# Even weight tiles, second products at the pair's end, and a last output block copied and stored in halves, in a fused GEGLU feed-forward kernel

## The chip, the cores and the metric

The kernel runs on one core of one Trainium2 chip. The metric is the time of one execution on the device in microseconds (us). Times are given as the median of several runs. A profile is one execution recorded by the hardware profiler; its times count from the start of the span.

## The reference

```python
B, S, D, F = 32, 32, 1024, 3584        # all bf16
def _gelu(x):
    return jax.nn.gelu(x, approximate=True)
def reference(x, w_gate, w_up, w_down):   # x: (B, S, D), w_gate and w_up: (D, F), w_down: (F, D)
    return (_gelu(x @ w_gate) * (x @ w_up)) @ w_down
```

With the batch flattened, x has N = 1024 rows. There are two stages: a hidden matrix h of 3584 x 1024 (stored transposed, 28 tiles of 128 rows, in `hT`), and the product with `w_down`.

## The kernel before

**Building blocks.** A small scheduler (`_Program`) collects the instructions of all engines. It works out which instruction must wait for which: by 256-byte cells of the on-chip buffers, and for PSUM by bank. In `add` (line 52) a reader of a PSUM bank also waits for earlier readers of that bank on other engines:

```python
            if key[0] == "ps":
                for d in self.readers.get(key, ()):
                    if d.eng != eng:
                        deps[d.index] = d
```

TensorE (PE) runs its matmuls in the order in which the program lists them. The other engines' instructions, and the DMA issues of each queue, are sorted by a planned time `at`, which is only a sort key: each one then runs as soon as the one before it and the semaphores it waits for allow. All instructions are recorded at one line of the helper `emit` (L117), so the profile's groups are told apart by tile and shape, not by line.

**Stage one.** Gate and up products (j = 0 and 1) are computed for one tile of 128 hidden columns at a time, in two halves of 512 rows of x. After a start phase (four tiles held in `first`, loaded as 1024-byte rows, from tile `F0` = 11), the work goes over 13 pairs p of a left and a right tile (`LEFT`, `RIGHT` = left + 15). Each pair uses a Strassen-like scheme with seven products instead of eight, each with j = 0 and 1, each of four matmuls of 128x128 by 128x512:

- products 1 and 2 use the weights and x as they are (bf16); the others use sums of blocks that VectorE, GpSimd and ScalarE prepare in fp32r (`sums_x` in buffer `S`, `sums_w` in buffer `T`);
- the order in a long pair (p from 4) is 1 1 5 2 2 6 6 5 7 3 7 3 4 4. The short pairs 0 to 3 (`EARLY`) have products 1 and 2 from the start phase (product 1's sums are kept in `kept`, inside tiles of `hT` not yet written) and run 5 5 6 6 7 3 7 3 4 4;
- the eight PSUM banks are A = (0, 1), E = (2, 3), B = (4, 5), C = (6, 7). Product 1 goes to A and is copied by ScalarE to B, where product 6 is added; B is copied to C, where product 7 is added, and so on. Product 5 goes to E and is copied to `p5`;
- GELU is ScalarE's (`act`); the adds and the products that write `hT` are VectorE's (`tt`, `glu`).

Weights of a pair of pairs (a group `gi`) are loaded by SP's queue into `raw[gi % 2]` (`load_pairs`: four DMAs, left and right, gate and up, 512-byte rows). The load of a group waits until all readers of the buffer two groups earlier are done. The last group has one tile on each side, so its rows have 256 bytes. The four `w_down` quarters (`load_wd`) take the place of x and weights later on.

**Stage two.** Seven sweeps of 56 matmuls in the order 1, 2, 7, 5, 6, 3, 4 use the same scheme with tiles 0 to 13 and 14 to 27 of `hT`; sweeps 1 and 2 are bf16, the others fp32r. Sweep 4 ends the kernel: its four blocks t of 128 rows lie in banks 0 to 3 (`PA`), and `done4` (line 554) copies them to `late`, ScalarE for even t and VectorE for odd t, and SP stores each (128 rows of 1024 bytes). SP waits for all stores at the end.

Of the kernel before, what the change touches and what calls it, by code (L numbers as in the profile page):

```python
# [6 lines left out]
P = 128  # L7
# [116 lines left out]
def bass_standalone__geglu_ffn__sampling_kernel(  # L124
# [21 lines left out]
    with ExitStack() as es:  # L146
# [54 lines left out]
        for n in [512] * 6 + [P] * 2:  # L201
            mm(3, one[:, 0:P], one[:, 0:n], True, True)

        NX, F0 = 2, 11
        for i, eng in enumerate(("sp", "act")):
            dma(eng, xn[:, 2 * i:2 * i + 2, :], x_r[:, 2 * i:2 * i + 2, 0:NX * P], 0, f"xn{i}")

        def load_first(eng, j, k0, k1, after=()):
            dma(eng, first[:, j, k0:k1, :], w_r[j][:, k0:k1, F0 * P:(F0 + 4) * P], 0, f"w0_{j}_{k0}", after)

        def load_x(h, k0, k1, after=()):
            pr.add("sp", "dma_start_transpose", xT[h][:, k0:k1, :], xf[h * 512:(h + 1) * 512, k0 * P:k1 * P],
# [17 lines left out]

        LEFT = [11, 12] + list(range(11))
        NP, EARLY = len(LEFT), 4

        def left(p): return LEFT[p]
        def right(p): return LEFT[p] + 15


        kept = [hT[:, m:m + 2, :].rearrange("p t n -> p (t n)").bitcast(FP32).rearrange("p (j n) -> p j n", j=2)  # L240
                for m in (7, 9, 22, 24)]


        SLOT = 0.905
        t0 = 32.7
        T0 = []
        for p in range(NP):
            T0.append(t0)
            t0 += (10 if p < EARLY else 13.9) * SLOT
        base = t0  # L250

        KO = 2
# [1 line left out]
        steps = [(m, j, k) for k in range(DK - KO) for j in range(2) for m in range(4)]  # L254
        for m in range(4):
            steps += [(m, j, k) for j in range(2) for k in range(DK - KO, DK)] + [(m, None, None)]
        for m, j, k in steps:
            if j is None:
                at = 17.0 + m * 0.87
                act(tmp[:, m, :], bank(2 * m), GELU, at)  # L260
                tt(hT[:, F0 + m, 0:512], tmp[:, m, :], bank(2 * m + 1), MUL, at)
                continue
            op = mm(2 * m + j, first[:, j, k, m * P:(m + 1) * P], xT[0][:, k, :], k == 0, k in (3, DK - 1), add=k > 3)
            if k == 3 and m < 2:
                act(kept[m][:, j, :], bank(2 * m + j), COPY, 10.5)
            if (m, j) == (3, 1):
                if k < 2:
                    load_first("act", 0, 2 * k + 4, 2 * k + 6, [op])
                    load_first("act", 1, 2 * k + 4, 2 * k + 6)
                if k == 3:  # L270
                    for k0 in range(0, DK, 2):
                        load_x(1, k0, k0 + 2, [op])
# [5 lines left out]
        for m, j, k in steps:  # L278
            if j is None:
                at = 25.0 + m * 0.87  # L280
                act(tmp[:, m, :], bank(2 * m), GELU, at)
                tt(hT[:, F0 + 2 + m, 512:1024], tmp[:, m, :], bank(2 * m + 1), MUL, at)
                continue
            mm(2 * m + j, first[:, j, k, (m + 2) * P:(m + 3) * P], xT[1][:, k, :], k == 0, k == DK - 1)


        def load_near(at):
# [1 line left out]
                dma("sp", near[:, j, :, :], w_r[j][:, :, right(0) * P:(right(1) + 1) * P], at, f"near{j}")  # L289

        def load_pairs(gi, s, at, ks=slice(0, DK)):
            n = min(2, NP - 2 * gi)
            for j in range(2):
                m = (left, right)[s](2 * gi)
                dma("sp", raw[gi % 2][:, s, j, ks, 0:n * P], w_r[j][:, ks, m * P:(m + n) * P], at, f"w{gi}_{j}{s}_{ks.start}")

        load_near(10)
        load_pairs(1, 0, 11, slice(0, 4))
# [7 lines left out]
        def pair_w(p, s, ks):  # L306
            col = slice((p % 2) * P, (p % 2 + 1) * P)
            if p < 2:
                return first[:, :, ks, col] if s == 0 else near[:, :, ks, col]
            return raw[(p // 2) % 2][:, s, :, ks, col]  # L310


# [53 lines left out]
        sums_w(0, 3, 28.6)  # L366
        t4 = sums_w(0, 4, 33.9)

        A, E, B, C = (0, 1), (2, 3), (4, 5), (6, 7)
        for p in range(NP):  # L370
            t0 = T0[p]
            if p % 2 == 0 and 2 <= p // 2 + 1 < (NP + 1) // 2:
                load_pairs(p // 2 + 1, 0, t0)
                load_pairs(p // 2 + 1, 1, t0)
            if p == 3:
                load_wd(0, 0, t0)
            if p == NP - 1:
                load_wd(0, 1, t0)
            ml, mr = left(p), right(p)
            at = lambda s: t0 + s * SLOT  # L380

            def product(n, j, b, start):
                for k in range(4):
                    if n < 3:
                        kk = k + 4 * (n - 1)
                        l, r = stat(p, j, kk), x0[:, kk, :]
                    else:
                        s, u = {3: (3, 3), 4: (4, 4), 5: (0, 0), 6: (1, 1), 7: (2, 2)}[n]
                        l, r = T[:, unit(p, u), j, k, :], S[:, 4 * s + k, :]
                    mm(b, l, r, start and k == 0, k == 3, add=not start)  # L390

            def glu(m, h, g, u, at_):
                tt(hT[:, m, h * 512:(h + 1) * 512], g, u, MUL, at_)

            p5 = [tmp[:, 0, :], tmp[:, 1, :]]
            g11, g12, g22, g21 = (tmp[:, i, :] for i in range(2, 6))

            if p < EARLY:
                o = -4
                for j in range(2):  # L400
                    act(bank(B[j]), kept[p][:, j, :], COPY, at(0.1 + j * 0.1))
                product(5, 0, E[0], True)
                act(p5[0], bank(E[0]), COPY, at(1))
                product(5, 1, E[1], True)
                product(6, 0, B[0], False)
                act(bank(C[0]), bank(B[0]), COPY, at(3))
                act(p5[1], bank(E[1]), COPY, at(3.1))
                product(6, 1, B[1], False)
                act(bank(C[1]), bank(B[1]), COPY, at(4))
            else:  # L410
                o = 0
                product(1, 0, A[0], True)
                act(bank(B[0]), bank(A[0]), COPY, at(1))
                product(1, 1, A[1], True)
                act(bank(B[1]), bank(A[1]), COPY, at(2))
                product(5, 0, E[0], True)
                act(p5[0], bank(E[0]), COPY, at(3))
                product(2, 0, A[0], False)
                act(g11, bank(A[0]), GELU, at(4))
                product(2, 1, A[1], False)  # L420
                glu(ml, 0, g11, bank(A[1]), at(5.2))
                product(6, 0, B[0], False)
                act(bank(C[0]), bank(B[0]), COPY, at(6))
                product(6, 1, B[1], False)
                act(bank(C[1]), bank(B[1]), COPY, at(7))
                product(5, 1, E[1], True)
                act(p5[1], bank(E[1]), COPY, at(8))
            u22 = bank(A[1] if p < EARLY - 1 else E[1])
            product(7, 0, C[0], False)
            tt(g22, bank(C[0]), p5[0], ADD, at(o + 9.1))  # L430
            act(g22, g22, GELU, at(o + 10))
            product(3, 0, B[0], False)
            tt(g12, bank(B[0]), p5[0], ADD, at(o + 10.1))
            act(g12, g12, GELU, at(o + 11))
            product(7, 1, C[1], False)
            tt(u22, bank(C[1]), p5[1], ADD, at(o + 11.1))
            glu(mr, 1, g22, u22, at(o + 11.9))
            product(3, 1, B[1], False)
            tt(bank(B[1]), bank(B[1]), p5[1], ADD, at(o + 12.1))
            glu(mr, 0, g12, bank(B[1]), at(o + 13))  # L440
            product(4, 0, C[0], False)
            act(g21, bank(C[0]), GELU, at(o + 13))
            product(4, 1, C[1], False)
            glu(ml, 1, g21, bank(C[1]), at(o + 14.1))
            if p + 1 < NP:
                sums_w(p + 1, 0, at(o + 9), "pool", [t4])
                if p + 1 < EARLY:
                    sums_w(p + 1, 1, at(o + 11.5))
                    sums_w(p + 1, 2, at(o + 14.3))
                    sums_w(p + 1, 3, at(o + 9.5))  # L450
                    t4 = sums_w(p + 1, 4, at(o + 14.4))
                else:
                    sums_w(p + 1, 1, at(o + 14.3))
                    sums_w(p + 1, 2, at(o + 12), "pool")
                    sums_w(p + 1, 3, at(o + 9.5))
                    t4 = sums_w(p + 1, 4, at(o + 20.5))


        KL, KR = list(range(14)), list(range(14, FM))
# [92 lines left out]
            out_dma(0, t, 1, late[:, 1, t, :])  # L552

        def done4(t, at):
            if t % 2:
                pr.add("dve", "tensor_copy", late[:, 2, t, :], bank(PA[t]), at=at)
            else:
                act(late[:, 2, t, :], bank(PA[t]), COPY, at)
            out_dma(1, t, 0, late[:, 2, t, :])
# [14 lines left out]
        with nc.Block() as block:  # L574
            for name, e in (("sync", "sp"), ("scalar", "act"), ("gpsimd", "pool"), ("tensor", "pe"), ("vector", "dve")):
                getattr(block, name)(lambda eng, e=e: pr.emit(
                    e, eng, sems, [("out", totals["out"])] if e == "sp" else ()))


# [26 lines left out]
```

## Time and profile before

| what | value |
|---|---|
| median of 7 runs | 276.02 us (275.46 to 276.25) |
| the profiled execution: its own time, its span | 275.69 us, 273.7 us |
| PE busy, matmuls | 270.0 us (99%), 1200 |
| VectorE, ScalarE, GpSimd busy | 189.7, 126.2, 45.5 us |
| granted TensorE clock | full in the whole span |
| matmuls of fp32r sums (S and T) | 800 |
| first fp32r matmul (pair 0) starts at | 32.64 us |
| pair 4 starts, pair 12 ends at | 69.58 us, 183.04 us |
| last matmul ends, last copy ends at | 270.87 us, 271.60 us |
| HBM read | 22.28 MB |

Matmuls are pipelined: the recorded duration of one (some 390 ns) is longer than the distance between two starts, so the length of a stage is read from starts, and a busy PE is not a PE at its peak. PEld are the weight loads that run beside the matmuls. Idle time of another engine costs nothing by itself.

### The profile page before, as it was taken

The page shows a single profiled execution, that of the slowest core. Times are in us where ns is not written, and L with a number is a line of the kernel's source. Part 1 is how long each engine was busy: PE and PEld are TensorE (multiplying, and loading weights), DVE is VectorE, ACT ScalarE, POOL GpSimd, SP SyncE. Part 2 cuts the span into 40 slices and gives each one's busy share as a digit, 9 for nine tenths or more (in the row PEclk, how much of TensorE's full clock was granted, in tenths as well). Part 3 has the DMA queues.
Part 4 walks back from the last instruction along what each step waited for, and adds up shares of the span by engine and source line. Part 5 has one row for each costly group of instructions (what it writes and reads, how often), then busy time and mean ns, then how long its engine had stood idle before and what let it go on. Part 6 is the DMA issues. An engine that isn't in the chain of part 4 may idle for free.

```text
span 273.7 us, 3259 instructions
## 1 busy us (share of the span) xinstructions
PE 270.0 (99%) x1200; PEld 187.4 (68%) x1200; DVE 189.7 (69%) x221; ACT 126.2 (46%) x195; POOL 45.5 (17%) x27
## 2 busy tenths in 40 slices
PE   8999999999999999999999999999999999999995
PEld 4444488888686767767686867674447888888884
DVE  1049978988665648374666666479972999999942
ACT  2353767567464555646454645531120112255561
POOL 1000032035060514325160606000000000000000
PEclk9999999999999999999999999999999999999999
DMA  7999511963800920193400007097011000001112
GB/s 178 275 187 301 134 33 53 282 211 108 199 2 0 244 63 2 39 268 78 78 2 0 0 0 263 7 317 223 0 38 38 0 2 0 0 0 61 38 57 77
DMA packets 46863, 26.42 MB, mean 97 GB/s; under 512 B 12544, under 2 KB 46848, under 8 KB 46848
## 3 DMA queue, kind: packets, MB, share of 16 engines
q1 hardware_dynamic: 44624, 24.25, 33.0%
q10 hardware_dynamic: 2224, 1.97, 2.8%
q8 instruction: 9, 0.15, 0.2%
q14 instruction: 6, 0.05, 0.1%
HBM read 22.28 MB, written 2.10 MB: 89 GB/s over the span
## 4 chain that ended last, share of the span: by engine, by line
PE 99%; DVE 0%; issue 0%
PE ps L117 99%; DVE arena L117 0%
## 5 line engine op out<-in xcount | busy, mean ns | idle before, releaser
L117 PE MATMUL ps<-S,T 128*128 128x512 f32 x520 | 125.5, 397 | 0.0
L117 PEld LDWEIGHTS ps<-S,T 128*128 128x128 f32 x520 | 97.4, 188 | 22.7 <-issue 0.8
L117 POOL TENSOR_TENSOR T<-arena 128x1024 fp32r<-128x1024 bf16 x21 | 44.8, 2152 | 122.4 <-DVE T L117 113.7
L117 ACT ACTIVATE tmp<-ps 128x512 f32<-128x512 f32 x64 | 38.2, 597 | 55.6 <-PE ps L117 55.6
L117 DVE TENSOR_TENSOR hT<-tmp,ps 128x512 bf16<-128x512 f32 x56 | 37.2, 685 | 38.2 <-PE ps L117 35.9
L117 PE MATMUL ps<-arena 128*128 128x512 bf16 x272 | 62.5, 381 | 0.1
L117 ACT ACTIVATE ps<-ps 128x512 f32<-128x512 f32 x52 | 30.3, 584 | 48.4 <-PE ps L117 48.4
L117 PE MATMUL ps<-T,S 128*128 128x512 f32 x224 | 51.3, 390 | 0.0
L117 DVE TENSOR_TENSOR T<-arena,T 128x1024 fp32r<-128x1024 bf16 x40 | 48.4, 1217 | 0.0
L117 PEld LDWEIGHTS ps<-T,S 128*128 128x128 f32 x224 | 42.0, 188 | 8.8
L117 PEld LDWEIGHTS ps<-arena 128*128 128x128 bf16 x272 | 24.8, 98 | 33.6 <-issue 3.4
L117 DVE TENSOR_TENSOR tmp<-ps,tmp 128x512 f32<-128x512 f32 x26 | 18.0, 692 | 21.7 <-PE ps L117 21.7
L117 DVE TENSOR_TENSOR T<-arena 128x1024 fp32r<-128x1024 bf16 x19 | 22.7, 1219 | 7.7 <-PE ps L117 7.4
L117 PE MATMUL ps<-arena,hT 128*128 128x512 bf16 x112 | 24.3, 379 | 0.0
L117 DVE TENSOR_TENSOR ps<-ps,tmp 128x512 f32<-128x512 f32 x30 | 20.9, 696 | 2.8 <-PE ps L117 2.8
L117 PEld LDWEIGHTS ps<-arena,hT 128*128 128x128 bf16 x112 | 10.9, 98 | 13.3 <-issue 0.3
L117 ACT ACTIVATE tmp<-tmp 128x512 f32<-128x512 f32 x26 | 16.4, 632 | 5.7 <-DVE tmp L117 4.6
L117 DVE TENSOR_TENSOR S<-hT 128x1024 fp32r<-128x1024 bf16 x14 | 16.6, 1218 | 0.0
L117 ACT ACTIVATE T<-arena 128x1024 fp32r<-128x1024 bf16 x13 | 13.7, 1053 | 0.0
L117 PE MATMUL ps<-S 128*128 128x512 f32 x56 | 12.9, 389 | 0.0
L117 PEld LDWEIGHTS ps<-S 128*128 128x128 f32 x56 | 10.5, 188 | 2.2
L117 ACT ACTIVATE S<-arena 128x1024 fp32r<-128x1024 bf16 x9 | 9.3, 1056 | 3.1 <-PE ps L117 3.0
(25 smaller groups left out, 62.0 us busy)
## 6 DMA issues: line engine op xcount, KB each, us to landing
arena<-in_w_down_dram SPq DMA_DIRECT2D x4, 1792.0 KB, 9.4
arena<-in_w_gate_dram SPq DMA_DIRECT2D x10, 512.0 KB, 5.9
arena<-in_w_up_dram SPq DMA_DIRECT2D x10, 512.0 KB, 6.7
out_dram<-arena SPq DMA_DIRECT2D x12, 128.0 KB, 1.7
arena<-in_w_gate_dram SPq DMA_DIRECT2D x4, 256.0 KB, 5.2
arena<-in_w_up_dram SPq DMA_DIRECT2D x4, 256.0 KB, 5.2
arena<-in_w_up_dram ACTq DMA_DIRECT2D x4, 128.0 KB, 4.7
arena<-in_w_gate_dram ACTq DMA_DIRECT2D x2, 256.0 KB, 4.9
```

What stands on the lines that cost most here:

```text
L117: ins = name(eng, *args, **kw) if callable(name) else getattr(eng, name)(*args, **kw)
```

## The change

Four things change:

1. The start phase takes tiles 0 to 3 instead of 11 to 14, and the pairs are renumbered so that every weight load starts at an even tile. The last pair is (14, 15), so that its left and right tiles come in one load of 512-byte rows for gate and one for up.
2. In pairs 4 to 11, product 2 with its GELU moves to the pair's end (`second`); A and E change places from one pair to the next. Pair 12 keeps product 2 where it was.
3. In the short pairs the order becomes 5 6 5 6 7 3 7 3 4 4. The planned times of copies and sums are written anew; the weight sum for product 4 has an earlier key in the long pairs.
4. In `done4` the last block (t = 3) is copied in two halves of 256 columns, the first by ScalarE and stored from ScalarE's queue, the second by VectorE and stored from SP's; SP waits for two semaphores at the end.

The core of the diff (the new names are `tile`, `move`, `second`, `short`, `last`):

```diff
-        LEFT = [11, 12] + list(range(11))
+        LEFT = [2, 3] + list(range(4, 14)) + [14]
+        RIGHT = [26, 27] + list(range(16, 26)) + [15]
...
-        def right(p): return LEFT[p] + 15
+        def right(p): return RIGHT[p]
...
-                for m in (7, 9, 22, 24)]
+                for m in (10, 12, 22, 24)]
...
-        SLOT = 0.905
-        t0 = 32.7
+        SLOT = 0.9064
+        t0 = 33.0
...
-        A, E, B, C = (0, 1), (2, 3), (4, 5), (6, 7)
+        B, C = (4, 5), (6, 7)
         for p in range(NP):
             t0 = T0[p]
+            short, last = p < EARLY, p == NP - 1
+            A, E = ((0, 1), (2, 3)) if short or (p - EARLY) % 2 == 0 else ((2, 3), (0, 1))
             if p % 2 == 0 and 2 <= p // 2 + 1 < (NP + 1) // 2:
                 load_pairs(p // 2 + 1, 0, t0)
-                load_pairs(p // 2 + 1, 1, t0)
+                if p < NP - 3:
+                    load_pairs(p // 2 + 1, 1, t0)
...
+            def second(at_):
+                product(2, 0, A[0], False)
+                act(g11, bank(A[0]), GELU, at_ + 0.95 * SLOT)
+                product(2, 1, A[1], False)
+                glu(ml, 0, g11, bank(A[1]), at_ + 2.2 * SLOT)
...
+            o = 4 if short else 7.8 if last else 5.9
+            if short:
                 for j in range(2):
                     act(bank(B[j]), kept[p][:, j, :], COPY, at(0.1 + j * 0.1))
...
+            else:
+                for j in range(2):
+                    product(1, j, A[j], True)
+                    move(A[j], B[j], at(0.95 * (j + 1)))
+            product(5, 0, E[0], True)
+            act(p5[0], bank(E[0]), COPY, at(o - 3))
+            if last:
+                second(at(2.9))
+            product(6, 0, B[0], False)
+            move(B[0], C[0], at(o - 2))
+            if short:
                 product(5, 1, E[1], True)
...
+            product(6, 1, B[1], False)
+            move(B[1], C[1], at(o - 1))
+            if not short:
                 product(5, 1, E[1], True)
-                act(p5[1], bank(E[1]), COPY, at(8))
+            act(p5[1], bank(E[1]), COPY, at(o - 0.9))
...
             glu(ml, 1, g21, bank(C[1]), at(o + 6.1))
+            if not short and not last:
+                second(at(o + 6))
...
-                    t4 = sums_w(p + 1, 4, at(o + 20.5))
+                    t4 = sums_w(p + 1, 4, T0[p + 1] + 4.4 * SLOT)
...
         def done4(t, at):
+            if t == 3:
+                for h, eng in enumerate(("act", "sp")):
+                    cut = slice(h * 256, (h + 1) * 256)
+                    if h:
+                        pr.add("dve", "tensor_copy", late[:, 2, t, cut], ps[:, PA[t], cut], at=at)
+                    else:
+                        act(late[:, 2, t, cut], ps[:, PA[t], cut], COPY, at)
+                    dma(eng, out_r[:, 4 + t, cut], late[:, 2, t, cut], end, "out" if h else "out2")
+                return
```

More of the change, by code (lines that the diff above doesn't have):

```diff
@@ L202, in bass_standalone__geglu_ffn__sampling_kernel @@
             mm(3, one[:, 0:P], one[:, 0:n], True, True)
-        NX, F0 = 2, 11
+        NX = 2
         for i, eng in enumerate(("sp", "act")):
@@ L208, in load_first @@
         def load_first(eng, j, k0, k1, after=()):
-            dma(eng, first[:, j, k0:k1, :], w_r[j][:, k0:k1, F0 * P:(F0 + 4) * P], 0, f"w0_{j}_{k0}", after)
+            dma(eng, first[:, j, k0:k1, :], w_r[j][:, k0:k1, 0:4 * P], 0, f"w0_{j}_{k0}", after)
         def load_x(h, k0, k1, after=()):
@@ L248, in bass_standalone__geglu_ffn__sampling_kernel @@
             T0.append(t0)
-            t0 += (10 if p < EARLY else 13.9) * SLOT
+            t0 += (10 if p < EARLY else 13.84) * SLOT
         base = t0
@@ L256, in bass_standalone__geglu_ffn__sampling_kernel @@
             steps += [(m, j, k) for j in range(2) for k in range(DK - KO, DK)] + [(m, None, None)]
+        tile = lambda m: (m + 2) % 4
         for m, j, k in steps:
@@ L260, in bass_standalone__geglu_ffn__sampling_kernel @@
                 act(tmp[:, m, :], bank(2 * m), GELU, at)
-                tt(hT[:, F0 + m, 0:512], tmp[:, m, :], bank(2 * m + 1), MUL, at)
+                tt(hT[:, tile(m), 0:512], tmp[:, m, :], bank(2 * m + 1), MUL, at)
                 continue
-            op = mm(2 * m + j, first[:, j, k, m * P:(m + 1) * P], xT[0][:, k, :], k == 0, k in (3, DK - 1), add=k > 3)
+            op = mm(2 * m + j, first[:, j, k, tile(m) * P:(tile(m) + 1) * P], xT[0][:, k, :], k == 0, k in (3, DK - 1), add=k > 3)
             if k == 3 and m < 2:
@@ L281, in bass_standalone__geglu_ffn__sampling_kernel @@
                 act(tmp[:, m, :], bank(2 * m), GELU, at)
-                tt(hT[:, F0 + 2 + m, 512:1024], tmp[:, m, :], bank(2 * m + 1), MUL, at)
+                tt(hT[:, m, 512:1024], tmp[:, m, :], bank(2 * m + 1), MUL, at)
                 continue
-            mm(2 * m + j, first[:, j, k, (m + 2) * P:(m + 3) * P], xT[1][:, k, :], k == 0, k == DK - 1)
+            mm(2 * m + j, first[:, j, k, m * P:(m + 1) * P], xT[1][:, k, :], k == 0, k == DK - 1)
         def load_near(at):
@@ L291, in load_pairs @@
         def load_pairs(gi, s, at, ks=slice(0, DK)):
-            n = min(2, NP - 2 * gi)
             for j in range(2):
                 m = (left, right)[s](2 * gi)
-                dma("sp", raw[gi % 2][:, s, j, ks, 0:n * P], w_r[j][:, ks, m * P:(m + n) * P], at, f"w{gi}_{j}{s}_{ks.start}")
+                dma("sp", raw[gi % 2][:, s, j, ks, :], w_r[j][:, ks, m * P:(m + 2) * P], at, f"w{gi}_{j}{s}_{ks.start}")
         load_near(10)
@@ L308, in pair_w @@
             if p < 2:
-                return first[:, :, ks, col] if s == 0 else near[:, :, ks, col]
+                return first[:, :, ks, slice((p + 2) * P, (p + 3) * P)] if s == 0 else near[:, :, ks, col]
+            if p == NP - 1:
+                return raw[0][:, 0, :, ks, slice(s * P, (s + 1) * P)]
             return raw[(p // 2) % 2][:, s, :, ks, col]
@@ L367, in bass_standalone__geglu_ffn__sampling_kernel @@
         t4 = sums_w(0, 4, 33.9)
-        A, E, B, C = (0, 1), (2, 3), (4, 5), (6, 7)
+        B, C = (4, 5), (6, 7)
         for p in range(NP):
             t0 = T0[p]
+            short, last = p < EARLY, p == NP - 1
+            A, E = ((0, 1), (2, 3)) if short or (p - EARLY) % 2 == 0 else ((2, 3), (0, 1))
             if p % 2 == 0 and 2 <= p // 2 + 1 < (NP + 1) // 2:
                 load_pairs(p // 2 + 1, 0, t0)
-                load_pairs(p // 2 + 1, 1, t0)
+                if p < NP - 3:
+                    load_pairs(p // 2 + 1, 1, t0)
             if p == 3:
                 load_wd(0, 0, t0)
-            if p == NP - 1:
+            if last:
                 load_wd(0, 1, t0)
@@ L390, in product, with move @@
                     mm(b, l, r, start and k == 0, k == 3, add=not start)
+            def move(a, b, at_):
+                act(bank(b), bank(a), COPY, at_)
             def glu(m, h, g, u, at_):
                 tt(hT[:, m, h * 512:(h + 1) * 512], g, u, MUL, at_)
+            def second(at_):
[3 more added lines that the diff above has]
+                glu(ml, 0, g11, bank(A[1]), at_ + 2.2 * SLOT)
@@ L395, in bass_standalone__geglu_ffn__sampling_kernel @@
             p5 = [tmp[:, 0, :], tmp[:, 1, :]]
             g11, g12, g22, g21 = (tmp[:, i, :] for i in range(2, 6))
-            if p < EARLY:
-                o = -4
+            o = 4 if short else 7.8 if last else 5.9
+            if short:
                 for j in range(2):
                     act(bank(B[j]), kept[p][:, j, :], COPY, at(0.1 + j * 0.1))
-                product(5, 0, E[0], True)
-                act(p5[0], bank(E[0]), COPY, at(1))
-                product(5, 1, E[1], True)
[L405 to L425, printed above, removed]
@@ new lines, in bass_standalone__geglu_ffn__sampling_kernel @@
+            else:
[4 more added lines that the diff above has]
+            act(p5[0], bank(E[0]), COPY, at(o - 3))
+            if last:
+                second(at(2.9))
+            product(6, 0, B[0], False)
+            move(B[0], C[0], at(o - 2))
+            if short:
+                product(5, 1, E[1], True)
+            product(6, 1, B[1], False)
+            move(B[1], C[1], at(o - 1))
@@ L426, in bass_standalone__geglu_ffn__sampling_kernel @@
+            if not short:
                 product(5, 1, E[1], True)
-                act(p5[1], bank(E[1]), COPY, at(8))
+            act(p5[1], bank(E[1]), COPY, at(o - 0.9))
             u22 = bank(A[1] if p < EARLY - 1 else E[1])
             product(7, 0, C[0], False)
-            tt(g22, bank(C[0]), p5[0], ADD, at(o + 9.1))
-            act(g22, g22, GELU, at(o + 10))
+            tt(g22, bank(C[0]), p5[0], ADD, at(o + 1.1))
+            act(g22, g22, GELU, at(o + 2))
             product(3, 0, B[0], False)
-            tt(g12, bank(B[0]), p5[0], ADD, at(o + 10.1))
@@ L434, in bass_standalone__geglu_ffn__sampling_kernel @@
-            act(g12, g12, GELU, at(o + 11))
+            tt(g12, bank(B[0]), p5[0], ADD, at(o + 2.1))
+            act(g12, g12, GELU, at(o + 3))
             product(7, 1, C[1], False)
-            tt(u22, bank(C[1]), p5[1], ADD, at(o + 11.1))
-            glu(mr, 1, g22, u22, at(o + 11.9))
+            tt(u22, bank(C[1]), p5[1], ADD, at(o + 3.1))
+            glu(mr, 1, g22, u22, at(o + 3.9))
             product(3, 1, B[1], False)
-            tt(bank(B[1]), bank(B[1]), p5[1], ADD, at(o + 12.1))
@@ L440, in bass_standalone__geglu_ffn__sampling_kernel @@
-            glu(mr, 0, g12, bank(B[1]), at(o + 13))
+            tt(bank(B[1]), bank(B[1]), p5[1], ADD, at(o + 4.1))
+            glu(mr, 0, g12, bank(B[1]), at(o + 5))
             product(4, 0, C[0], False)
-            act(g21, bank(C[0]), GELU, at(o + 13))
+            act(g21, bank(C[0]), GELU, at(o + 5))
             product(4, 1, C[1], False)
-            glu(ml, 1, g21, bank(C[1]), at(o + 14.1))
-            if p + 1 < NP:
-                sums_w(p + 1, 0, at(o + 9), "pool", [t4])
+            glu(ml, 1, g21, bank(C[1]), at(o + 6.1))
@@ L447, in bass_standalone__geglu_ffn__sampling_kernel @@
+            if not short and not last:
+                second(at(o + 6))
+            if not last:
+                sums_w(p + 1, 0, at(o + 1), "pool", [t4])
                 if p + 1 < EARLY:
[L448 to L451, printed above, removed]
-                else:
-                    sums_w(p + 1, 1, at(o + 14.3))
-                    sums_w(p + 1, 2, at(o + 12), "pool")
-                    sums_w(p + 1, 3, at(o + 9.5))
-                    t4 = sums_w(p + 1, 4, at(o + 20.5))
+                    sums_w(p + 1, 1, at(o + 3.5))
+                    sums_w(p + 1, 2, at(o + 6.3))
+                    sums_w(p + 1, 3, at(o + 1.5))
+                    t4 = sums_w(p + 1, 4, at(o + 6.4))
+                else:
+                    sums_w(p + 1, 1, at(o + 6.3))
+                    sums_w(p + 1, 2, at(o + 4), "pool")
+                    sums_w(p + 1, 3, at(o + 1.5))
+                    t4 = sums_w(p + 1, 4, T0[p + 1] + 4.4 * SLOT)
@@ L576, in bass_standalone__geglu_ffn__sampling_kernel @@
                 getattr(block, name)(lambda eng, e=e: pr.emit(
-                    e, eng, sems, [("out", totals["out"])] if e == "sp" else ()))
+                    e, eng, sems, [(n, totals[n]) for n in ("out", "out2")] if e == "sp" else ()))
 _INS = ['x', 'w_gate', 'w_up', 'w_down']
```

## The prediction

> **What bounds the kernel now.** I read the page first, for busy shares and the chain that ended last:
>
> ```profile
> PE 270.0 (99%) x1200; PEld 187.4 (68%) x1200; DVE 189.7 (69%) x221; ACT 126.2 (46%) x195; POOL 45.5 (17%) x27
> ...
> PE 99%; DVE 0%; issue 0%
> ```
>
> TensorE is the chain, so an edit counts only where it shortens the row of 1,200 matmuls or what follows the last one. The program issues 1,200 matmuls before and after. What can change is the distance from one start to the next. For that I asked for windows cut at starts that I counted off in program order (40 matmuls in each of pairs 0 to 3, 56 in each later pair and each sweep; the view's counts hold a straddler or two more). Columns: window, length, then busy time of PE, PEld, DVE, ACT, POOL, granted clock, DMA share, GB/s.
>
> ```profile
> 42.03:51.21 9.18, 9.18 (x41) 7.43 (x40) 7.97 (x11) 6.02 (x11) 2.15 (x1) 1.00 0.36 97
> 82.18:94.79 12.61, 12.61 (x58) 8.92 (x57) 7.63 (x11) 6.93 (x11) 4.26 (x2) 1.00 0.42 109
> 183.03:195.13 12.10, 12.10 (x57) 5.50 (x57) 12.10 (x12) 1.75 (x3) 0.00 (x0) 1.00 0.55 178
> 219.93:232.63 12.70, 12.70 (x57) 10.51 (x56) 12.70 (x12) 2.40 (x4) 0.00 (x0) 1.00 0.00 0
> ```
>
> The last two rows are sweeps of one type: 12.10 / 56 = 0.2160 us per bf16 matmul, 12.70 / 56 = 0.2267 us per fp32r one, at full clock. Against these rates a short pair (40 fp32r) should take 9.07 us and takes 9.18: 0.11 too much. A long pair (16 bf16, 40 fp32r) should take 3.456 + 9.068 = 12.52 and takes 12.61: 0.08 too much. To place both excesses I read PE's timeline of pair 5 (start, length to the last end, count):
>
> ```profile
> 82.18 1.90 PE L117 MATMUL ps<-arena 128*128 128x512 bf16 x8
> 83.73 1.27 PE L117 MATMUL ps<-S,T 128*128 128x512 f32 x4
> 84.84 1.90 PE L117 MATMUL ps<-arena 128*128 128x512 bf16 x8
> 86.39 8.55 PE L117 MATMUL ps<-S,T 128*128 128x512 f32 x36
> 94.79 0.39 PE L117 MATMUL ps<-arena 128*128 128x512 bf16 x1
> ```
>
> Read the starts, not the lengths: 1.55, 1.11, 1.55 and 8.40 us. There is no idle time here; each change of type costs some nanoseconds. In pair 1 it is different. From the timelines of PE's weight loads, ScalarE and VectorE:
>
> ```profile
> 45.65 1.22 PEld L117 LDWEIGHTS ps<-S,T 128*128 128x128 f32 x6 [0.25 <-issue]
> ...
> 44.95 0.58 ACT L117 ACTIVATE ps<-ps 128x512 f32<-128x512 f32 x1 [0.46 <-PE ps L117]
> ...
> 43.85 1.22 DVE L117 TENSOR_TENSOR T<-arena 128x1024 fp32r<-128x1024 bf16 x1
> ```
>
> The weight load of matmul 16 of the pair (product 7, first half) would be due at 45.44, when matmul 15 starts, and comes at 45.65. ScalarE's copy of bank B[0] to C[0] ended at 45.53, and PE waited for it. VectorE's sum for product 7 had ended at 45.07.
>
> **Part 1: order in the short pairs (a gain of 0.45 us).** The copy to C[0] follows product 6, first half. Before, that is the third product of five and matmul 16 stands right behind the fourth. After, the order is 5, 6, 5, 6, 7, so product 6 ends one product (0.907 us) earlier and its copy is put ahead of the second half of 5. In pair 1's times: product 6 ends at 44.01; ScalarE's two queued copies (out of `kept` to B[1], 43.37 to 43.97, and p5, from 43.91) let it start by about 44.40; it ends at 44.98, and the load is due at 45.44. The wait goes, and with it 0.113 us in each of the four pairs (9.180 - 40 x 0.2267; pair 0 shows the same pause): **-0.45**. What is late next: VectorE's sum (45.07), with 0.3 us to spare, since VectorE's run of work behind product 7 hangs on PE and moves with it. Product 6 is also one product nearer to the `kept` copy into B[0]: that ends at 42.42, the load is due at 42.72, 0.2 to 0.3 us to spare (in pair 0: 33.26 against 33.51). What ScalarE does later, p5 and the GELU behind it, slips by some 0.4 us; VectorE's product with that GELU comes after an add and a weight sum and does not reach PE.
>
> **Part 2: second products last in the long pairs (-0.21).** Pairs 4 to 11 now run two halves of product 1 (bf16), 40 fp32r, two halves of product 2 (bf16); the next pair goes on in bf16. One run of four fp32r matmuls goes. Its price from the starts above: 1.11 - 4 x 0.2267 = +0.204 at the fp32r side, 1.55 - 8 x 0.2160 = -0.178 at the bf16 side, so 0.026 us net. The long run's own price, 8.40 - 36 x 0.2267 - 0.178 = 0.06, stays. Eight pairs: **-0.21**. Pair 12 keeps its order.
>
> Is a wait added? In the new order, from a pair's start: the copy of A[0] to B[0] ends at 1.66 us (after before's rows, 83.26 + 0.58 - 82.18) and product 6 wants it at 2.5; the copy to C[0] ends near 4.4 and product 7 wants it at 5.2; A[0] has been idle since 1.66 when product 2 adds to it at 10.9. Because A and E change places, the next pair's product 1 writes banks that were last read near 9.7 by VectorE, 2.9 us earlier; its E is this pair's A, last read by the GELU (to 12.6) and by the product with it (to about 13.7), wanted at 14.3 and at 17.1. Each has at least 0.8 us.
>
> Moved DMAs: left tiles are now read until the pair's end, so SP's loads of the groups wait longer, and the right tiles' loads queue behind them on SP. Before, the group for pairs 8 and 9 was issued at 88.77 to 90.86 and landed by 98.04. After, it starts near 94 and lands near 104. GpSimd's sums for pair 8 cannot start before pair 7 does (107.4). Covered by 3 us and more; two later groups are alike, and the last is one load of 512-byte rows per matrix instead of two of 256. The `w_down` half loaded at 164.3 moves to about 170 and still lands (8 us) long before its use near 193; the other two are freed about 1 us earlier. **0**.
>
> **Part 3: even tiles (0).** The aligned group loads landed 1.81 us apart (92.75 and 94.56 for tiles 6 and 7), the odd-aligned ones behind them 1.80 and 1.68 apart (96.36, 98.04). 1024-byte packets took 46 ns in the first loads (odd start) and 46 to 48 in the aligned `w_down`. Nothing to gain, and pairs 4 on hide these loads anyway. A pause that loads do cause, 0.26 us near 8.5 us, ends with the transposed x, which is not touched.
>
> **Part 4: the last block in halves (+0.05).** VectorE's copy is last now, then a store:
>
> ```profile
> 270.00 0.60 ACT L117 ACTIVATE arena<-ps 128x512 bf16<-128x512 f32 x1 [1.22 <-PE ps L117]
> 270.91 0.69 DVE L117 CAST arena<-ps 128x512 bf16<-128x512 f32 x1 [1.12 <-PE ps L117]
> ...
> out_dram<-arena SPq DMA_DIRECT2D x12, 128.0 KB, 1.7
> ```
>
> The halves do not run side by side: in `add`, a reader of a PSUM bank waits for earlier readers on other engines (lines 66 to 69), and both halves lie in bank 3. So ScalarE copies, then VectorE. By the slope between 512 and 1024 elements (ScalarE 0.597 and 1.056, VectorE 0.685 and 1.217) a half takes 0.37 and 0.42, an estimate; bounds 0.30 to 0.60 and 0.29 (a 256-element bf16 copy, 291 ns in the groups of instructions) to 0.69. With 0.03 between engines: 0.37 + 0.03 + 0.42 = 0.82 against 0.69, **+0.13**. The last store is 64 KB: an engine's eight packets at 27 ns (512-byte loads) instead of 46, 0 to -0.15, I take **-0.12**. SP has one more semaphore to wait for and ScalarE issues beside SP: 0 to +0.15, I take **+0.04**, the nearer end, since SP sits idle when ScalarE issues. Whole tail **+0.05**, bounds -0.22 to +0.8.
>
> The Trainium skill, page "PSUM — Partial Sum Buffer", section "PSUM bank collisions raise a hardware error": two engines may not read one bank at once, disjoint columns included, so a side-by-side copy is no option; no run here shows one. Had it been one, the copy would end at 0.42 and the sum would be about -1.0.
>
> The Trainium skill, page "DMA: Bandwidth & Descriptors", section "Anatomy of one DMA", fits a GpSimd-queue transfer as about 2.0 us plus bytes / 436 GB/s, an estimate of 2.3 us for 128 KB; the row has 1.7. Its second term alone would make a half store an estimated 0.15 shorter, and the sum -0.64.
>
> **Sum.** -0.45 - 0.21 + 0.05 = **-0.61 us**. The profiled execution took 275.69 (span 273.72 + 1.97), 0.33 under the median of seven. The same step on the median 276.02 gives **275.41**; the profiled span should become 273.11.
>
> **Rivals.** (a) The pause stays in the short pairs: VectorE's sum or the `kept` copy becomes the last to arrive, margins of 0.2 to 0.3 us. For it: they are the thinnest margins here. Against: both hang on PE and move with it. Then -0.61 + 0.45 = -0.16: 275.86. (b) The tail at its bad bound: fixed costs dominate and half copies are nearly as long as whole ones. -0.66 + 0.4 to 0.8: 275.76 to 276.16. Against: both engines show a slope. (c) Slower: in the long pairs ScalarE's FIFO, where the GELU of product 2 now stands just ahead of the next pair's moves out of A, delays the copy to B[0], and PE waits at product 6 in eight pairs. It decides when that copy ends more than 0.8 us late. Each 0.1 us beyond is +0.8; at 1.0 us late, 8 x 0.2 - 0.61 = +1.0: 277.0. Against: that GELU ends by 12.6 of a 12.6 us pair, and the move cannot begin before 1.08 of the next. (d) The change does not do what it says: halves run in series and even tiles land no sooner. It is in my sum.
>
> **Chances.** Forecast 0.60; (a) 0.20, (b) 0.15, (c) 0.05. A measurement here can tell about 0.2%, 0.55 us, so faster means below 275.47. The forecast lies just beyond that, and its own spread (the tail, the scatter of runs) puts 0.09 of its 0.60 on the near side: faster 0.51, same 0.09 + 0.20 + 0.15 = 0.44, slower 0.05. Range: 275.05 (tail near its good bound, -0.27 from its forecast, and scatter) to 275.95 (past (a), half of (b)).
>
> **What would show it.** Short pairs of 9.07 us with no weight load idle before product 7; long pairs of 12.58 us with starts 3.28 (16 bf16) and 9.30 (40 fp32r) apart; ScalarE's half copy, then VectorE's, 0.8 us in all after the last matmul; loads for pairs 8 and 9 issued near 94. I am wrong if short pairs still take 9.18, if a long pair takes more than 12.61, or if the tail from last matmul to span end exceeds 2.9 us (now 2.85) by more than 0.3.

## The result and the profile after

The changed kernel takes 275.25 us (median of 25 runs, 274.48 to 276.66), the kernel before 276.13 (61 runs). The ratio is 0.9967, 95% interval 0.9959 to 0.9976: -0.91 us, between -1.13 and -0.66. It is faster, by a third of a per cent. The time lies inside the forecast range; the forecast gain of 0.61 lies just outside the interval, on its small side.

The page of the changed kernel, busy time and chain:

```profile
span 273.2 us, 3284 instructions
...
PE 269.2 (99%) x1200; PEld 188.0 (69%) x1200; DVE 188.9 (69%) x221; ACT 126.0 (46%) x196; POOL 45.4 (17%) x27
...
PE 96%; DMA 2%; SPq 0%; issue 0%; DVE 0%; ACT 0%; DVEq 0%
```

TensorE is still the chain; the 2% of DMA are the 6.1 us in which a load of transposed x was on its way in the start phase, and PE stood idle for only 0.19 us of that time, from 8.32 to 8.51. The same windows as before, pair 1 and a long pair (6), cut at their first matmuls (window, length, busy time of PE, PEld, DVE, ACT, POOL, clock, DMA share, GB/s):

```profile
42.10:51.16 9.06, 9.06 (x41) 7.51 (x40) 7.96 (x11) 5.86 (x11) 2.17 (x1) 1.00 0.36 95
94.43:106.99 12.56, 12.56 (x57) 8.99 (x56) 7.54 (x11) 6.93 (x11) 4.25 (x2) 1.00 0.66 168
```

A short pair took 9.18 and takes 9.07 (9.067 from the starts, the window is rounded); a long pair took 12.61 and takes 12.56. PE's timeline of the changed kernel shows the two long runs per pair:

```profile
92.69 3.63 PE L117 MATMUL ps<-arena 128*128 128x512 bf16 x16
95.97 9.44 PE L117 MATMUL ps<-S,T 128*128 128x512 f32 x40
105.25 2.55 PE L117 MATMUL ps<-arena 128*128 128x512 bf16 x11
```

The starts are 3.28 and 9.28 us apart. In pair 1 the weight loads no longer pause before product 7 (it starts near 45.7), and ScalarE's copy to C[0], the one at 44.45, ends at 45.04, before its load is due at 45.50. First PEld's timeline, then ScalarE's:

```profile
41.87 4.72 PEld L117 LDWEIGHTS ps<-S,T 128*128 128x128 f32 x21
```

```profile
41.88 0.60 ACT L117 ACTIVATE ps<-hT 128x512 f32<-128x512 f32 x1
43.43 0.60 ACT L117 ACTIVATE ps<-hT 128x512 f32<-128x512 f32 x1 [0.95 <-DVE hT L117]
43.97 0.58 ACT L117 ACTIVATE tmp<-ps 128x512 f32<-128x512 f32 x1
44.45 0.59 ACT L117 ACTIVATE ps<-ps 128x512 f32<-128x512 f32 x1
```

The end, from the timeline. The last matmul ends at 270.22:

```profile
270.26 0.38 ACT L117 ACTIVATE arena<-ps 128x256 bf16<-128x256 f32 x1 [0.31 <-PE ps L117]
270.68 0.37 ACTq L117 DMA_DIRECT2D out_dram<-arena  x1
270.75 0.42 DVE L117 CAST arena<-ps 128x256 bf16<-128x256 f32 x1 [1.60 <-ACT arena L117]
```

VectorE's half waits for ScalarE's; the span ends later after the last matmul than before.

**Where the time went.** The stages of one execution repeat to some 0.04 us from one run to the next, all but the start phase. This table therefore carries more than the totals do. Short pairs: first matmul of pair 0 to first of pair 4. Long pairs: to the first of sweep 1. Tail: end of the last matmul to the start of the last recorded instruction (the span's end is 0.05 later; the expectations below mean the same stretch when they say "to the span's end"). The seven sweeps take 87.84 us in every complete trace. In the traces marked * some matmul records are missing at the same places, which adds 0.21 to the short stage; there 37.15 is the unchanged value. (The weight loads are complete in every trace: the four short pairs take 36.95 to 36.96 us by them before and in e2 to e4, 36.49 to 36.53 with the new order, e7 aside.)

| kernel | short pairs | long pairs | tail | ratio to before (95%) |
|---|---|---|---|---|
| before | 36.94 | 113.46 | 2.80 | |
| changed | 36.51 | 113.09 | 2.91 | 0.9967 (0.9959 to 0.9976) |
| changed, again (e11) | 36.49 | 113.09 | 2.91 | 0.9967 (0.9953 to 0.9982) |
| e1, short pairs' order alone | 36.71* | 113.46 | 2.80 | 0.9980 (0.9967 to 0.9993) |
| e2, second products last alone | 37.15* | 113.09 | 2.81 | 0.9992 (0.9981 to 1.0002) |
| e3, halves alone | 37.15* | 113.46 | 2.89 | 1.0001 (0.9988 to 1.0014) |
| e4, even tiles alone | 37.15* | 113.46 | 2.84 | 1.0006 (0.9993 to 1.0018) |
| e5, changed without halves | 36.71* | 113.09 | 2.83 | 0.9971 (0.9960 to 0.9982) |
| e6, changed, last copy whole by ScalarE | 36.70* | 113.09 | 2.74 | 0.9973 (0.9959 to 0.9987) |
| e12, e6 again | 36.47 | 113.09 | 2.73 | 0.9963 (0.9947 to 0.9979) |
| e7, changed, sum for product 7 later | 38.99* | 113.09 | 2.91 | 1.0057 (1.0042 to 1.0072) |
| e8, changed, one more round trip | 36.72* | 113.29 | 2.91 | 0.9980 (0.9965 to 0.9995) |
| e9, changed, product 2 in the middle | 36.50 | 113.41 | 2.91 | one run |
| e10, changed, two stores of one copy | 36.50 | 113.09 | 2.94 | 0.9979 (0.9963 to 0.9995) |

The start of pair 0 is not in the table because it scatters: 32.64 before, 32.79 changed, and 33.13, 32.49, 32.81, 32.19 in e11, e12, e10 and e9, which do not differ from the changed kernel up to there. In e8, which does not either, it is 33.93. That is 1.74 us of scatter in a stage that waits for loads. By the stages the change is worth -0.43 - 0.37 + 0.11 = -0.69 us.

### The profile page after: what moved, and what is told of

Its sections match the earlier page's. It is cut to its first block, busy times and chain, and to the rows that moved or that the text cites. A ratio compares the mean times of both kernels' runs of the same rounds, so it can differ in the third digit from the quotient of the medians.

```text
span 273.2 us, 3284 instructions
## 1 busy us (share of the span) xinstructions
PE 269.2 (99%) x1200; PEld 188.0 (69%) x1200; DVE 188.9 (69%) x221; ACT 126.0 (46%) x196; POOL 45.4 (17%) x27
## 4 chain that ended last, share of the span: by engine, by line
PE 96%; DMA 2%; SPq 0%; issue 0%; DVE 0%; ACT 0%; DVEq 0%
PE ps L117 96%; DMA arena<-in_x_dram 2%; SPq L117 0%; DVE arena L117 0%; ACT arena L117 0%; DVEq L115 0%
## 5 line engine op out<-in xcount | busy, mean ns | idle before, releaser
L117 PE MATMUL ps<-S,T 128*128 128x512 f32 x520 | 122.0, 393 | 0.0
L117 PE MATMUL ps<-arena 128*128 128x512 bf16 x272 | 61.2, 379 | 0.2 <-DMA arena<-in_x_dram 0.2
```

The source lines that it names most:

```text
L117: ins = name(eng, *args, **kw) if callable(name) else getattr(eng, name)(*args, **kw)
```

## Experiments

### The four parts alone, each put into the kernel before

**e1, the order in the short pairs.**

```diff
                 product(5, 0, E[0], True)
                 act(p5[0], bank(E[0]), COPY, at(1))
-                product(5, 1, E[1], True)
                 product(6, 0, B[0], False)
-                act(bank(C[0]), bank(B[0]), COPY, at(3))
-                act(p5[1], bank(E[1]), COPY, at(3.1))
+                act(bank(C[0]), bank(B[0]), COPY, at(2))
+                product(5, 1, E[1], True)
                 product(6, 1, B[1], False)
-                act(bank(C[1]), bank(B[1]), COPY, at(4))
+                act(bank(C[1]), bank(B[1]), COPY, at(3))
+                act(p5[1], bank(E[1]), COPY, at(3.1))
```

> Only the order in the short pairs (5 6 5 6 7 ...) is taken into the kernel before. Theory (a wait for ScalarE's copy to C[0]): pairs 1 to 3 go from 9.18 to 9.07 us, the idle weight load before product 7 is gone, nothing else moves; time -0.45 us (ratio 0.9984). Rival (the next late arrival, VectorE's sum or the copy out of kept, takes the wait over): short pairs stay between 9.1 and 9.18, time -0.2 to 0.

Measured: short pairs 36.71* against 37.15*, -0.44 us, and -0.55 (-0.91 to -0.19) by the ratio. PEld's timeline across the place where it paused:

```profile
42.00 5.17 PEld L117 LDWEIGHTS ps<-S,T 128*128 128x128 f32 x23
```

One line, no idle time in it. The theory holds and nothing took the wait over.

**e2, second products last**, with the alternation of A and E and the planned times that go with it:

```diff
                 product(5, 0, E[0], True)
                 act(p5[0], bank(E[0]), COPY, at(3))
-                product(2, 0, A[0], False)
-                act(g11, bank(A[0]), GELU, at(4))
-                product(2, 1, A[1], False)
-                glu(ml, 0, g11, bank(A[1]), at(5.2))
+                if last:
+                    second(at(2.9))
...
             glu(ml, 1, g21, bank(C[1]), at(o + 14.1))
+            if not short and not last:
+                second(at(o + 14))
```

> Only the second products' move to the end of pairs 4 to 11, with the alternation of A and E, is taken into the kernel before. Theory (one round trip between the two types less, nothing waits): by the prediction's term 12.58 us per pair and -0.21 us in all; by the profile of the changed kernel 12.56 per pair and -0.37. Rival (the moved DMAs, which now start some 5 us later, or the alternation of banks make PE wait): a pair over 12.6 us, time no better than before.

Measured: long pairs 113.09 against 113.46: -0.37, pairs of 12.56. The ratio's -0.22 (-0.52 to +0.06) does not separate the two sizes, the stage does. The pause of the short pairs is there as before (PEld's timeline):

```profile
41.87 3.59 PEld L117 LDWEIGHTS ps<-S,T 128*128 128x128 f32 x16
45.71 1.45 PEld L117 LDWEIGHTS ps<-S,T 128*128 128x128 f32 x7 [0.25 <-issue]
```

So the two gains are independent (-0.44 and -0.37 alone, -0.43 and -0.37 together), and neither the later loads nor the exchanged banks make PE wait.

**e3, the halves.** The diff is that of `done4` in the change, and SP's second wait.

> Only the last block's halves are taken into the kernel before. Theory (the halves run in series): from the last matmul's end to the span's end 2.91 us instead of 2.80, time +0.1 us. Rival (a shorter store and a second queue pay for it): 2.8 us or less, time 0 to -0.2.

Measured: tail 2.89 against 2.80, +0.09; by the ratio no difference (-0.33 to +0.39). The timeline shows the series again:

```profile
270.83 0.38 ACT L117 ACTIVATE arena<-ps 128x256 bf16<-128x256 f32 x1 [0.31 <-PE ps L117]
271.25 0.37 ACTq L117 DMA_DIRECT2D out_dram<-arena  x1
271.32 0.42 DVE L117 CAST arena<-ps 128x256 bf16<-128x256 f32 x1 [1.60 <-ACT arena L117]
```

**e4, the even tiles** (`LEFT`, `RIGHT`, the tiles of `first`, one load for the last group):

> Only the even tiles (start phase at tile 0, pairs renumbered, last group in one load) are taken into the kernel before. Theory (packets cost the same from an odd and an even start): pair 0 starts within the scatter of the start phase around 32.7 us, all pairs as before, time 0 within 0.2 us. Rival (aligned rows land earlier in the start phase, where PE waits for loads; this would make up for the 0.2 us by which the timed gain exceeds what the stages of the two profiles add up to): time -0.2 us or more.

Measured: ratio 1.0006, -0.19 to +0.50 us; all pairs as before, and the tail of 2.84 within its scatter. The rival's gain of 0.2 or more lies at or outside the interval's end. Even tiles alone bring nothing that can be seen.

### What bounds the short pairs next

**e7** puts VectorE's weight sum for product 7 behind the one for product 4, in the changed kernel:

```diff
-                    sums_w(p + 1, 2, at(o + 6.3))
+                    sums_w(p + 1, 2, at(o + 6.5))
```

> The changed kernel with VectorE's weight sum for product 7 placed behind that for product 4 in the short pairs (1.2 us later). Theory (with the wait for ScalarE's copy gone this sum is the next late arrival, with some 0.3 us to spare): PE waits 0.75 to 1.0 us at product 7 in pairs 1 to 3, +2.3 to 3.0 us against the changed kernel. Rival (there is much more slack, the sum is not next): no change, short pairs stay at 9.07.

Measured: short pairs 38.99* against 36.71*: +2.28 us, 0.76 per pair, at the low end of the theory. VectorE's and PEld's timelines:

```profile
43.88 1.22 DVE L117 TENSOR_TENSOR T<-arena,T 128x1024 fp32r<-128x1024 bf16 x1
45.02 1.22 DVE L117 TENSOR_TENSOR T<-arena 128x1024 fp32r<-128x1024 bf16 x1
```

```profile
46.29 8.98 PEld L117 LDWEIGHTS ps<-S,T 128*128 128x128 f32 x40 [0.86 <-DVE T L117]
```

The sum ends at 46.24 and the load comes at 46.29, released by VectorE. In the changed kernel VectorE's row of the same sum is:

```profile
43.91 1.22 DVE L117 TENSOR_TENSOR T<-arena 128x1024 fp32r<-128x1024 bf16 x1
```

Against that the sum came 1.14 us later from the pair's start, and PE lost 0.76, so its slack in the changed kernel is about 0.38 us (it ends at 45.13 there, the load is due at 45.50). Of ScalarE's copy to C[0] and this sum, the sum is now the later one, with the margin that the prediction had put at 0.3. By the rows another margin is thinner: the copy out of `kept` to B[0] ends at 42.48, and the load of product 6 is due at 42.78 (four loads after the pair's first at 41.87), 0.30 us later. No run here moved that copy.

### What a round trip between the types costs

A round trip is the way from bf16 matmuls to a run of fp32r matmuls and back. Its price is what the starts show beyond the distances inside sweeps of one type.

**e8** puts the first half of product 2 ahead of the second half of product 4: runs of 36 and 4 fp32r instead of 40.

```diff
+            split = not short and not last
+            if split:
+                product(2, 0, A[0], False)
             product(4, 1, C[1], False)
...
             glu(ml, 1, g21, bank(C[1]), at(o + 6.1))
-            if not short and not last:
-                second(at(o + 6))
+            if split:
+                product(2, 1, A[1], False)
+                glu(ml, 0, g11, bank(A[1]), at(o + 8.2))
```

> The changed kernel with the first half of product 2 placed ahead of the second half of product 4 in pairs 4 to 11: one round trip between the types more per pair, with a run of four fp32r matmuls, the same work. Theory by the stages of the two profiles: a round trip costs 0.045 to 0.047 us, a pair 12.61 instead of 12.56, +0.37 us in all. Rival (the prediction's term): 0.026 us, a pair 12.59, +0.21 us.

Measured: long pairs 113.29 against 113.09, +0.207 us in eight pairs: 0.026 each, the rival's size. But it does not lie where the rival has it. PEld's timeline of one pair, in which no load is missing:

```profile
109.72 8.13 PEld L117 LDWEIGHTS ps<-S,T 128*128 128x128 f32 x36
118.10 0.55 PEld L117 LDWEIGHTS ps<-arena 128*128 128x128 bf16 x4 [0.26 <-issue]
118.77 0.88 PEld L117 LDWEIGHTS ps<-S,T 128*128 128x128 f32 x4
119.91 0.33 PEld L117 LDWEIGHTS ps<-arena 128*128 128x128 bf16 x3 [0.27 <-issue]
```

From start to start, unrounded, the run of 36 takes 8.387 us and the run of four 1.145. In the kernel before, the loads of its runs of 36 and of four take 8.419 and 1.133. The run of four is dearer here than there, the run of 36 cheaper.

**e9** puts product 2 behind product 5's second half:

```diff
             act(p5[1], bank(E[1]), COPY, at(o - 0.9))
+            if not short and not last:
+                second(at(o - 0.1))
+                o = 7.9
...
-            if not short and not last:
-                second(at(o + 6))
```

> The changed kernel with product 2 of pairs 4 to 11 placed between product 5's second half and product 7: two fp32r runs of 16 and 24 matmuls per pair instead of one of 40. It asks what the price of a round trip hangs on: 0.026 us for the runs of four, 0.041 for the 40 that begin with product 5, 0.058 for the 36 that begin with product 6. If on the run's length: 0.041 to 0.058 each, a pair 12.60 to 12.64 us. If product 6 alone is dear: two of 0.041, a pair 12.60. If every added run costs what the short ones do: 12.586.

Measured: long pairs 113.41, +0.320 in eight: 0.040 per pair. PE's timeline:

```profile
95.44 4.00 PE L117 MATMUL ps<-S,T 128*128 128x512 f32 x16
99.28 1.90 PE L117 MATMUL ps<-arena 128*128 128x512 bf16 x8
100.83 5.82 PE L117 MATMUL ps<-S,T 128*128 128x512 f32 x24
106.49 1.69 PE L117 MATMUL ps<-arena 128*128 128x512 bf16 x7
```

The prices of all round trips, with the distances inside the sweeps (0.2158 us for bf16, 0.2267 for fp32r). In the changed kernel, for example, the run of 40 takes 9.283 us, 0.216 more than 40 such distances, and the 16 bf16 matmuls take 3.277, 0.176 less than 16 of theirs: 0.040 net.

| fp32r matmuls in the run | begins with | kernel | price, us |
|---|---|---|---|
| 4 | product 5 | before | 0.028 |
| 4 | product 4, second half | e8 | 0.039 |
| 16 | product 5 | e9 | 0.040 |
| 24 | product 7 | e9 | 0.040 |
| 36 | product 6 | before | 0.059 |
| 36 | product 5 | e8 | 0.028 |
| 40 | product 5 | changed | 0.040 |

Their sums give the pairs: 0.087 before, 0.040 changed, 0.067 in e8 and 0.080 in e9 over 12.52. The price goes neither by the run's length (36: 0.028 and 0.059) nor by the product that it begins with (product 5: 0.028 and 0.040). What sets it stays open. So e8's added trip costs what the removed trip did in sum, but it does not show that any run of four has that price.

### The tail

**e5** takes the halves out of the changed kernel; **e6** and, again, **e12** have ScalarE copy the last block whole; **e10** also stores that copy in two halves from the two queues; **e11** is the changed kernel again.

```diff
 # e5 (SP's second wait goes too)
-            if t == 3:
...
-                return
             if t % 2:
```

```diff
 # e6, e12 (SP's second wait goes too)
-            if t == 3:
...
-                return
-            if t % 2:
+            if t == 1:
```

```diff
 # e10
             if t == 3:
+                act(late[:, 2, t, :], bank(PA[t]), COPY, at)
                 for h, eng in enumerate(("act", "sp")):
                     cut = slice(h * 256, (h + 1) * 256)
-                    if h:
-                        pr.add("dve", "tensor_copy", late[:, 2, t, cut], ps[:, PA[t], cut], at=at)
-                    else:
-                        act(late[:, 2, t, cut], ps[:, PA[t], cut], COPY, at)
                     dma(eng, out_r[:, 4 + t, cut], late[:, 2, t, cut], end, "out" if h else "out2")
```

> The changed kernel with the last block copied whole by VectorE and stored by SP, as before. Theory (the halves cost, since the second copy waits for the first): from the last matmul to the span's end 2.80 us instead of 2.91, all else as in the changed kernel, so about 0.1 us faster than it: -0.8 us against the kernel before by the stages (ratio 0.997). Rival (the halves pay): 2.9 us or more.

> The changed kernel with the last block copied whole by ScalarE (0.60 us in its rows, VectorE 0.69) and stored by SP. Theory (the tail is copy, issue, store in series): 2.71 us from the last matmul to the span's end, 0.2 less than the changed kernel; -0.9 us against the kernel before (ratio 0.9967). Rival (ScalarE is late from its copy of the block before): 2.8 us or more.

> The changed kernel with the last block copied whole by ScalarE, and stored in two halves, one from ScalarE's queue and one from SP's. Theory (a half store lands 0.12 us earlier than a whole one, and the two are issued side by side): 2.62 us from the last matmul to the span's end, 0.3 less than the changed kernel. Rival (two issues at once are slower, as at the kernel's start, where they take 0.46 to 0.49 us instead of 0.33, or the stores share the DMA engines): 2.74 us or more, no better than one store.

> The changed kernel once more, beside the others on one chip: tail 2.91 us, short pairs together 0.44 and long pairs 0.37 less than before; against the kernel before -0.7 us by these stages (ratio 0.9974), or -0.9 (0.9967) if the first measurement's surplus is real.

> The changed kernel with the last block copied whole by ScalarE and stored whole by SP, once more: tail 2.74 us, 0.17 less than the changed kernel, -0.87 us against the kernel before (ratio 0.9968). If the tail did not count in the time, the same as the changed kernel.

Tails: 2.91 changed, 2.83 without halves, 2.74 and 2.73 with ScalarE's whole copy. So the halves cost some 0.1 (0.08 to 0.11 by the kernels compared), and ScalarE's whole copy saves 0.17 to 0.18 against them. The end of e12:

```profile
269.02 0.60 ACT L117 ACTIVATE arena<-ps 128x512 bf16<-128x512 f32 x1 [1.22 <-PE ps L117]
269.93 0.60 ACT L117 ACTIVATE arena<-ps 128x512 bf16<-128x512 f32 x1 [0.31 <-PE ps L117]
```

ScalarE is idle for 0.31 us ahead of the last copy, so it is in time for it. Two stores of one copy gave 2.94 us, 0.2 more than one store: the theory fell and the rival holds. The two half stores of e10, the last column from issue to landing:

```profile
out_dram<-arena SPq DMA_DIRECT2D x1, 64.0 KB, 1.7
out_dram<-arena ACTq DMA_DIRECT2D x1, 64.0 KB, 1.9
```

The store of the whole block in e12 lands 1.7 us after its issue, and the halves of the changed kernel, issued 0.52 us apart, 1.6. Of two halves issued in the same moment, the one from ScalarE's queue takes 1.9. The issues took 0.33 and 0.37 us, as in the changed kernel, so slower issues are not the reason; which part of the path the two stores share was not tried.

The kernel of e6 and e12 is by its stages the best version. It beats the kernel before clearly (ratios 0.9973 and 0.9963); against the changed kernel its 0.17 to 0.18 us show in the stages and are too small for the times (0.9967, with overlapping intervals).

## Why the prediction was right, point by point

The direction and the range held: 275.25 in 275.05 to 275.95. The forecast itself, 275.41, stood on the median 276.02 of seven runs; over 61 runs that median is 276.13. By its own steps:

- **Short pairs: -0.45 forecast, -0.43 measured** (-0.44 alone in e1). The wait was ScalarE's copy to C[0]; the copy ended at 45.04 where 44.98 plus the 0.06 us later start of the pair was worked out. Both arrivals that were named as next did not become late; e7 measured the slack of one of them, VectorE's sum.
- **Long pairs: -0.21 forecast, -0.37 measured.** The mechanism was right (one round trip less, no wait added), the term was mis-sized. The step that failed is "The long run's own price, 8.40 - 36 x 0.2267 - 0.178 = 0.06, stays". It did not stay: the long run costs 0.059 before and 0.040 after. The removed short trip was sized nearly rightly (0.026 against 0.028). Together that is 0.047 per pair (12.607 to 12.560), times eight. Why the long run became cheaper is open. The prediction's rate of 0.2160 for bf16 holds the change of type at the sweep's start; inside the sweep it is 0.2158, which moves its prices by some 0.002.
- **Moved DMAs: 0, as forecast.** The loads for pairs 8 and 9 were issued at 93.88 to 95.92 and landed by 103.2 (forecast 94 and 104); no weight load of the pairs waits for a DMA.
- **Even tiles: 0, as forecast** (e4).
- **Tail: +0.05 forecast, +0.11 measured.** The halves took 0.38 and 0.42 (forecast 0.37 and 0.42) and the half store landed 0.12 sooner (forecast 0.12). Mis-sized was the step "with 0.03 between engines": VectorE waits for two semaphores, ScalarE's and PE's, and started 0.10 us after ScalarE's end. For SP's second wait the sum had 0.04, a choice inside a bound; it cost nothing visible.
- **Rivals.** (a) and (c) did not come: short pairs take 9.07 us and long pairs 12.56. (b) did not come: a half copy takes 0.38 of 0.60 us on ScalarE and 0.42 of 0.69 on VectorE. (d) is true: the halves run in series and cost time, and the even tiles gain nothing.

The stages make -0.69 where -0.61 was forecast. That they come so close is in part luck: 0.16 too little in the long pairs is partly made up by 0.06 too little loss in the tail. The timed -0.91 (-1.13 to -0.66) is 0.2 larger, but its interval reaches the stages' sum. Inside the span the start phase is the only stage that could hold more; it scatters by 1.74 us, e4 found no gain there, and e1 to e4 add up to -0.0021, about -0.58 us. That the change also shortens the start phase is not shown.

## What to carry to other kernels

When one engine is busy 99% of the span, cut the trace at that engine's own instruction starts and compare each stage with the best rate seen for the same instructions: here the excess was 0.11 us in a short pair and 0.08 to 0.09 in a long one. The first could be traced to one copy; of the second it is shown where it lies, not what sets it. A stage that repeats to some hundredths of a microsecond shows what the total time cannot. An instruction that feeds the next step should stand one step earlier than its consumer's turn, and the next late arrival should be sought before the gain is booked. Splitting a last copy over two engines cost time where the program lets them read one after the other; here the shorter of the two whole copies was better, and splitting its store over two queues was worse.

## What the runs showed of the hardware that was not expected

- Going from bf16 to fp32r matmuls and back cost 0.028 to 0.059 us, and neither the fp32r run's length nor the product that it begins with settles which.
- Two 64 KB stores issued at the same moment from two queues landed 1.7 and 1.9 us after issue (e10); one of 128 KB took 1.7 (e12).
- VectorE started 0.10 us after ScalarE's end where it had two semaphores to wait for, against 0.03 from the end of a last copy to the issue of its store.
